# Polysketch attention and a top-2 router: plain scatters to a row per pair, one pass of sums, four blocks of the largest expert last

## The chip, the cores and the metric

One Trainium2 chip, one of its cores. The metric is the device time of one execution in microseconds (us); lower is better. Engines are named as in the profile: PE (TensorE), DVE (VectorE), ACT (ScalarE), POOL (GpSimd, which also issues the indirect DMAs), SP (SyncE, which issues the loads).

## The reference, cut to what matters

```python
x = polysketch_attention(q, k, v, S1, S2)         # 4 batches, 4 heads, 1088 tokens -> x [N=4352, D=128]
noisy = x @ w_gate + log1p(exp(x @ w_noise)) * noise          # [4352, E=8]
top2, top2_w = two largest per token, softmax over the two
out = zeros(N, D)
for e in range(8):                                # w1[e] is 128x1024, w2[e] is 1024x128, all float32
    for k in range(2):
        mask = top2[:, k] == e
        out[mask] += top2_w[mask, k] * (relu(x[mask] @ w1[e]) @ w2[e])
```

Each token sends two (token, expert) pairs, 8,704 in all, and a token's output is the sum of its two pairs' results.

## The kernel before, in words

The kernel has two stages. In the first, `attention` runs over the four batches, and after each group of four tiles of 128 tokens `router` picks the two experts of every token. For each pair it works out a row of the DRAM table `xs` (each expert has a region of its own there) and scatters 128 rows at a time to it: the token's input times its weight, and the token's number as a 129th word. Those are 68 indirect DMAs on POOL's queue (line 433), each of 128 rows of 516 bytes.

In between, `table` counts the pairs of each expert and cuts them into 27 large blocks (256 rows) and 21 small ones (128 rows). `ends` writes 128 filler rows behind each expert's last pair (eight DMAs on SP, line 518), whose token numbers point at 128 spare rows of the result.

In the second stage `blocks` works through the 48 blocks: large and small in turn 21 times, then six large ones. For each, `fetch` loads on SP the rows (`xb`, line 526) and the expert's two weight matrices (`w`, 512 KB each, lines 529 and 530), whichever expert it is; the pool behind these tiles has five buffers. `block_input` transposes the rows (line 545), line 584 makes `hp = w1.T x`, `evict` applies relu on ACT and DVE in turn (`h`, lines 537 and 539), and `second` (line 559) accumulates `acc = h.T w2`, two groups behind. `second` then copies `acc` to `y` and issues one or two scatters (line 568), each of which adds 128 rows of `y` to the rows of `total` that the 129th words of `xb` name. Two such scatters can hit the same row, so the program puts each behind the landing of the one before. An `xb` buffer is free again only when the scatter that reads its 129th words has landed. Before the first of the last six blocks stores its result, line 564 copies `total` to `out`, and the last 12 scatters add to `out` itself.

A scheduler (the tile framework) sets the order on each engine. It inserts the waits from what each instruction reads and writes. DMAs of one kind take eight semaphores in turn (DMASW0 to 7 for POOL's, DMAHW0 to 7 for SP's and ACT's), and a DMA that takes a semaphore waits for the DMA that had it eight DMAs before.

Of the kernel before, what the change touches and what calls it, by code (L numbers as in the profile page):

```python
# [8 lines left out]
F32 = mybir.dt.float32  # L9
# [12 lines left out]
def kernel(  # L22
# [49 lines left out]
    wpool = ctx.enter_context(tc.tile_pool(name="wpool", bufs=5))  # L72
    dram = ctx.enter_context(tc.tile_pool(name="dram", bufs=1, space=DRAM))
# [125 lines left out]
    for e in range(E):  # L199
        nc.gpsimd.memset(base[:, e:e + 1], float(e * CAP))  # L200
    token = const.tile([P, TILES], I32, name="token")
    nc.gpsimd.iota(token[:, 0:B * NT].rearrange("p (b t) -> p b t", b=B),
                   pattern=[[S, B], [1, NT]], base=0, channel_multiplier=NT)
    for c in range(2):
        nc.gpsimd.iota(token[HALF * c:HALF * (c + 1), B * NT:TILES], pattern=[[2 * S, 2]],
                       base=SM + S * c, channel_multiplier=1)
# [3 lines left out]

    pad = const.tile([P, XW], F32, name="pad")
    nc.gpsimd.memset(pad[:], 0.0)
    nc.gpsimd.iota(pad[:, D:XW].bitcast(I32), pattern=[[0, 1]], base=N, channel_multiplier=1)
    total = dram.tile([N + P, D], F32, name="total", tag="total")

    def clear():

        for r0 in range(0, N + P, 2 * P * 8):
            n = min(2 * P * 8, N + P - r0)
            nc.scalar.dma_start(total[r0:r0 + n, :].rearrange("(p r) d -> p (r d)", p=P),  # L220
                                zeros[:, 0:n * D // P])
        for c in range(2):
            nc.scalar.dma_start(xs[E * CAP + P * c:E * CAP + P * (c + 1), :], pad[:])
# [120 lines left out]
    def router(x, n, t0):  # L344
# [76 lines left out]
        for i, g in enumerate((g1, g2)):  # L421
# [6 lines left out]
            nc.gpsimd.tensor_copy(xg[:, 0:n, D:XW].bitcast(I32), token[:, t0:t0 + n].unsqueeze(2))  # L428
# [3 lines left out]
            for t in range(n):  # L432
                nc.gpsimd.indirect_dma_start(  # L433
                    out=xs[:], out_offset=bass.IndirectOffsetOnAxis(ap=to[:, t:t + 1], axis=0),
                    in_=xg[:, t, :], in_offset=None)


    def table():
# [27 lines left out]
        full = shifted("full", cnt, 8)  # L466
# [5 lines left out]
        V.scalar_tensor_tensor(out=left[:], in0=big[:], scalar=-2.0 * P, in1=cnt, op0=ALU.mult, op1=ALU.add)  # L472
        V.tensor_scalar_add(left[:], left[:], P - 1.0)
        rest_ = shifted("rest", left[:], 7)
        which = const.tile([1, NK], F32, name="which")
        first_row = const.tile([1, NK], F32, name="first_row")
        number = row("number", NB)
        num_i = row("num_i", NB, I32)
        nc.gpsimd.iota(num_i[:], pattern=[[1, NB]], base=0, channel_multiplier=0)
        V.tensor_copy(number[:], num_i[:])  # L480
        for name, lo, n, size, x in (("b", 0, NB, 2 * P, big), ("s", NB, NS, P, rest_)):
            end = sums("end" + name, x)
            past = row("past" + name, n * E)
            p3 = past[:].rearrange("p (i e) -> p i e", e=E)
            V.tensor_tensor(out=p3, in0=number[:, 0:n].unsqueeze(2).to_broadcast([1, n, E]),
                            in1=end[:, 1:E + 1].unsqueeze(1).to_broadcast([1, n, E]), op=ALU.is_ge)
            V.tensor_reduce(out=which[:, lo:lo + n], in_=p3, axis=AX.X, op=ALU.add)

            step = row("step" + name, E)
            V.tensor_scalar(out=step[:], in0=x[:], scalar1=-float(size), scalar2=float(CAP), op0=ALU.mult, op1=ALU.add)  # L490
            if name == "s":
                V.scalar_tensor_tensor(out=step[:], in0=big[:], scalar=-2.0 * P, in1=step[:], op0=ALU.mult, op1=ALU.add)
                V.scalar_tensor_tensor(out=step[:, 0:E - 1], in0=big[:, 1:E], scalar=2.0 * P, in1=step[:, 0:E - 1], op0=ALU.mult, op1=ALU.add)
            V.tensor_tensor(out=p3, in0=p3, in1=step[:].unsqueeze(1).to_broadcast([1, n, E]), op=ALU.mult)
            V.tensor_reduce(out=first_row[:, lo:lo + n], in_=p3, axis=AX.X, op=ALU.add)
            V.scalar_tensor_tensor(out=first_row[:, lo:lo + n], in0=number[:, 0:n], scalar=float(size),
                                   in1=first_row[:, lo:lo + n], op0=ALU.mult, op1=ALU.add)

        V.tensor_scalar(out=left[:, 0:1], in0=big[:, 0:1], scalar1=2.0 * P, scalar2=None, op0=ALU.mult)
        V.tensor_scalar(out=first_row[:, NB:NK], in0=first_row[:, NB:NK], scalar1=left[:, 0:1], scalar2=None, op0=ALU.add)  # L500
        V.tensor_scalar(out=first_row[:], in0=first_row[:], scalar1=float(E * CAP), scalar2=None, op0=ALU.min)
        V.tensor_scalar(out=which[:], in0=which[:], scalar1=float(E - 1), scalar2=None, op0=ALU.min)
        tab = const.tile([1, 2 * NK + E], I32, name="tab")
# [3 lines left out]
        V.tensor_tensor(out=tab[:, 2 * NK:2 * NK + E], in0=cnt, in1=base[0:1, :], op=ALU.add)  # L507
# [4 lines left out]

    def ends(tab):
        for e in range(E):
            at = 2 * (NB + NS) + e
            r = nc.values_load(tab[0:1, at:at + 1], engines=SP, min_val=0, max_val=E * CAP - P,
                               skip_runtime_bounds_check_because=IN_RANGE)
            nc.sync.dma_start(xs[bass.ds(r, P), :], pad[:])

    def fetch(tab, k, n):  # L520
        e = nc.values_load(tab[0:1, 2 * k:2 * k + 1], engines=SP, min_val=0, max_val=E - 1,
                           skip_runtime_bounds_check_because=IN_RANGE)
        r = nc.values_load(tab[0:1, 2 * k + 1:2 * k + 2], engines=SP, min_val=0, max_val=E * CAP,
                           skip_runtime_bounds_check_because=IN_RANGE)
        xb = wpool.tile([P, 2, XW], F32, name="xb", tag="xb")
        nc.sync.dma_start(xb[:, 0:n, :], xs[bass.ds(r, P * n), :].rearrange("(c p) d -> p c d", p=P))
# [4 lines left out]
        return xb, w1, w2  # L531
# [18 lines left out]
    def blocks(tab, order, copy_at):  # L550
        later, copied = [], []

        def second():
            acc, h, w2, n, js, j0, xb, to = later.pop(0)
# [7 lines left out]
            if j0 + js == FJ:  # L562
                if to is out and not copied:
                    copied.append(nc.scalar.dma_start(out, total[0:N, :]))
                y = moe.tile([P, 2 * D], F32, name="y", tag="y")
                evict(y[:, 0:D * n], acc[:, 0:D * n])
                for c in range(n):
                    nc.gpsimd.indirect_dma_start(  # L568
                        out=to[:], out_offset=bass.IndirectOffsetOnAxis(ap=xb[:, c, D:XW].bitcast(U32), axis=0),
                        in_=y[:, D * c:D * (c + 1)], in_offset=None, compute_op=ALU.add)  # L570

        data = [fetch(tab, *order[0])]
        xTs = [block_input(data[0][0], order[0][1])]
        for s_, (k_, n) in enumerate(order):
            xb, w1, w2 = data.pop(0)
            xT = xTs.pop(0)
            if s_ + 1 < len(order):
                data.append(fetch(tab, *order[s_ + 1]))
            acc = ps_o.tile([P, 2 * D], F32, name="acc", tag="acc")
            js = 4 // n  # L580
            for j0 in range(0, FJ, js):
# [6 lines left out]
                later.append((acc, h, w2, n, js, j0, xb, out if s_ >= copy_at else total))  # L588
# [76 lines left out]
```

## Time and profile before

| | |
|---|---|
| median of 2 runs | 794.75 us (792.77 to 796.72) |
| the profiled execution | 801.78 us, its span 800.1 us |
| PE busy | 498.1 us, 62% of the span, granted clock 0.799 of full speed on the mean |
| POOL, DVE, ACT busy | 212.6, 192.4 and 119.1 us |
| DMA | 77.25 MB, mean 97 GB/s |

The profiled execution has its own time; shares and places below are of its span. A DMA-issuing instruction on POOL is shown with the time POOL spends on it, not with the time until its data has landed. Idle time of an engine counts only where that engine is on the path that sets the end.

### The profile page before, as it was taken

How to read it: one execution, taken by the hardware profiler on the slowest of the kernel's cores; microseconds unless marked ns; L12 is line 12 of the kernel's file. 1: busy time of each engine (PE TensorE's matmuls, PEld its weight loads, DVE VectorE, ACT ScalarE, POOL GpSimd, SP SyncE). 2: the span in 40 equal slices, each digit the busy share in tenths (PEclk: the TensorE clock that was granted, in tenths of full speed). 3: DMA queues.
4: the chain of work that ended last, by engine and by line, in shares of the span. 5: the costliest groups of instructions: out<-in, count | busy, mean ns of one | idle time of the engine just before them, and what ended most of it. 6: DMA issues, size and time to landing. Idle time of an engine off the chain costs nothing. (4 is left out here: it accounts for less than half of the span.)

```text
span 800.1 us, 8013 instructions
## 1 busy us (share of the span) xinstructions
PE 498.1 (62%) x2781; PEld 422.4 (53%) x2781; DVE 192.4 (24%) x664; ACT 119.1 (15%) x232; POOL 212.6 (27%) x233
## 2 busy tenths in 40 slices
PE   1485585678557555009966667777667776771970
PEld 1363473465355333009966666666656765661960
DVE  2114513341441435402211111211111111110210
ACT  0112202301221222001211111111111111110110
POOL 3101332423233042301322223232232223222233
PEclk9995556655655655558999999999999999996895
DMA  7600100000000000028566565556556455656621
GB/s 187 224 28 4 46 14 17 17 17 17 10 23 24 0 23 21 27 84 235 133 158 148 145 162 129 130 140 160 134 136 175 127 129 138 162 138 164 188 30 17
DMA packets 95128, 77.25 MB, mean 97 GB/s; under 512 B 11632, under 2 KB 87536, under 8 KB 94768
## 3 DMA queue, kind: packets, MB, share of 16 engines
q1 hardware_dynamic: 74688, 62.12, 27.7%
q0 software_dynamic: 12976, 9.42, 7.6%
q10 hardware_dynamic: 7424, 5.21, 2.1%
q8 instruction: 22, 0.36, 0.2%
q14 instruction: 18, 0.15, 0.1%
HBM read 64.36 MB, written 14.59 MB: 99 GB/s over the span
## 5 line engine op out<-in xcount | busy, mean ns | idle before, releaser
L584 PE MATMUL hp<-bT,w 128*128 128x256 f32 (+1 forms) x768 | 165.2, 349 | 35.3 <-DMA w<-in_moe_w_dram 34.1
L568 POOL DMA_INDIRECT total<-y,xb x63 | 98.1, 1557 | 296.8 <-issue 108.3
L559 PE MATMUL acc<-w,h 128*128 128x128 f32 x1200 | 164.1, 282 | 16.1 <-ACT h L539 16.1
L559 PEld LDWEIGHTS acc<-w,h 128*128 128x128 f32 x1200 | 160.2, 198 | 22.5 <-ACT h L539 16.5
L584 PEld LDWEIGHTS hp<-bT,w 128*128 128x128 f32 x768 | 120.8, 200 | 48.1 <-issue 24.3
L433 POOL DMA_INDIRECT xs<-xg,to x68 | 68.3, 1005 | 169.0 <-DMA xs<-xg,to 80.7
L537 DVE TENSOR_SCALAR h<-hp 128x512 f32<-128x512 f32 x80 | 55.3, 692 | 232.6 <-PE hp L584 231.4
L545 PE MATMUL bank<-ident,xb 128*128 128x128 f32 x75 | 18.8, 310 | 98.9 <-DMA xb<-xs 98.9
L539 ACT ACTIVATE h<-hp 128x512 f32<-128x512 f32 x70 | 41.8, 597 | 227.8 <-PE hp L584 205.4
L545 PEld LDWEIGHTS bank<-ident,xb 128*128 128x128 f32 x75 | 9.0, 145 | 105.9 <-DMA xb<-xs 70.2
L415 PE MATMUL bank<-masks,earlier 128*128 128x32 f32 (+1 forms) x18 | 5.4, 394 | 62.9 <-DVE g L407 62.9
L415 PEld LDWEIGHTS bank<-masks,earlier 128*128 128x128 f32 x18 | 4.5, 310 | 63.6 <-issue 63.6
L316 PE MATMUL bank<-qT,sq 128*128 128x512 f32 (+1 forms) x36 | 30.9, 955 | 9.8 <-ACT qT L314 9.7
L284 PE MATMUL bank<-vaug,phk 128*128 128x66 f32 x128 | 29.3, 424 | 12.3 <-DVE phk L229 12.3
L235 PE MATMUL bank<-sk,kT 128*128 128x64 f32 x136 | 29.8, 419 | 9.0 <-ACT kT L270 8.5
L284 PEld LDWEIGHTS bank<-vaug,phk 128*128 128x128 f32 x128 | 27.9, 330 | 13.4 <-issue 9.8
L235 PEld LDWEIGHTS bank<-sk,kT 128*128 128x128 f32 x136 | 29.6, 333 | 9.7 <-ACT kT L270 8.9
L537 DVE COPY bT<-bank 128x256 f32<-128x256 f32 x21 | 8.9, 425 | 104.6 <-PE bank L545 104.6
L568 POOL DMA_INDIRECT out_dram<-y,xb x12 | 18.7, 1555 | 43.8 <-issue 26.3
L317 PE MATMUL bank<-qT,sq 128*128 128x512 f32 (+1 forms) x36 | 28.3, 883 | 0.0
L321 DVE TENSOR_TENSOR phq<-qa,bank 128x512 f32<-128x512 f32 (+1 forms) x18 | 11.8, 658 | 61.0 <-PE bank L317 61.0
L330 PEld LDWEIGHTS bank<-kv,phq 128*128 128x128 f32 (+1 forms) x144 | 17.9, 198 | 11.2 <-DVE phq L321 5.1
(157 smaller groups left out, 388.1 us busy)
## 6 DMA issues: line engine op xcount, KB each, us to landing
w<-in_moe_w_dram SPq DMA_DIRECT2D x96, 512.0 KB, 5.2
xb<-xs SPq DMA_DIRECT2D x27, 129.0 KB, 2.2
out_dram<-total ACTq DMA_DIRECT2D x1, 2176.0 KB
kld<-in_k_dram SPq DMA_DIRECT2D x4, 512.0 KB, 6.9
vld<-in_v_dram SPq DMA_DIRECT2D x4, 512.0 KB, 5.0
qld<-in_q_dram SPq DMA_DIRECT2D x4, 512.0 KB, 6.0
total<-zeros ACTq DMA_DIRECT2D x2, 1024.0 KB
xb<-xs SPq DMA_DIRECT2D x21, 64.5 KB
```

Source lines behind the costliest of these rows:

```text
L235: nc.tensor.matmul(ps[:, c0:c0 + H * 2 * R], lhsT=kT, rhs=sk[:, i, :], start=(i == 0), stop=(i == 1))
L284: nc.tensor.matmul(o, lhsT=phk[:, t, hs, :].rearrange("p h f -> p (h f)"), rhs=vaug[:, hs, t, :], start=(t == 0), stop=False)
L316: nc.tensor.matmul(pa[:, 0:w], lhsT=sq[:, 0, :], rhs=qT[:, 0:w], start=True, stop=True)
L317: nc.tensor.matmul(pb[:, 0:w], lhsT=sq[:, 1, :], rhs=qT[:, 0:w], start=True, stop=True)
L330: nc.tensor.matmul(ps[rows, c0:c0 + 2 * A1], lhsT=phq[hp][:, P * i + rows.start:P * i + rows.stop], rhs=kv[:, hp, :], start=True, stop=True)
L433: nc.gpsimd.indirect_dma_start(out=xs[:], out_offset=bass.IndirectOffsetOnAxis(ap=to[:, t:t + 1], axis=0), in_=xg[:, t, :], in_offset=None)
L537: nc.vector.tensor_scalar_max(o, i, 0.0) if relu else nc.vector.tensor_copy(o, i)
L539: nc.scalar.activation(out=o, in_=i, func=AF.Relu) if relu else nc.scalar.copy(o, i)
L545: nc.tensor.transpose(ps[:, P * c:P * (c + 1)], xb[:, c, 0:D], ident[:])
L559: nc.tensor.matmul(acc[:, D * c:D * (c + 1)], lhsT=h[:, P * (n * i + c):P * (n * i + c + 1)], rhs=w2[:, j, :], start=(j == 0 and c == 0), ...
L568: nc.gpsimd.indirect_dma_start(out=to[:], out_offset=bass.IndirectOffsetOnAxis(ap=xb[:, c, D:XW].bitcast(U32), axis=0), in_=y[:, D * c:D * ...
L584: nc.tensor.matmul(hp[:, P * n * i:P * n * (i + 1)], lhsT=w1[:, P * (j0 + i):P * (j0 + i + 1)], rhs=xT[:, 0:P * n], start=True, stop=True)
```

## The change

- The pairs' rows in `xs` now carry the pair's number (twice the token's, plus 0 or 1) in place of the token's. Every pair's result has a row of its own in a DRAM table `parts` of 8,704 rows, so the scatters of `y` are plain writes, declared free of each other; a row number past the table (filler rows) is dropped. The router's scatters to `xs` and the filler rows are declared free of each other too.
- `clear` now zeroes all of `parts`, 8,704 rows (five DMAs, 4.46 MB) in place of 4,480 rows of `total` (three DMAs, 2.29 MB).
- `table` finds the expert with the most pairs (`star`) and sets its first 1,024 rows aside as four large blocks; the rest is cut into 23 large and 21 small ones. The four are last in the order, and their weights are loaded once.
- When the first of the four is through, `combine` adds the two rows of each token in seven chunks of 5 rows a partition (SP loads `two`, DVE adds, SP stores `one` to `out`), and the four blocks' eight scatters add to `out` behind that.
- `xb` and `y` have pools of eight buffers of their own.

```diff
-    total = dram.tile([N + P, D], F32, name="total", tag="total")
+    parts = dram.tile([PAIRS, D], F32, name="parts", tag="parts")
+    def disjoint(group, i):
+        if group in groups:
+            tc.declare_no_dep(i.ins, group=group, reason="rows of their own")
+        tc.add_to_no_dep_group(group, i.ins)
+        groups.setdefault(group, []).append(i.ins)
+    def behind(i, group):
+        for w in groups[group]:
+            tc.add_manual_dep(i.ins, w.name, SYNC, reason="reads what they write")
...
     def clear():
-        for r0 in range(0, N + P, 2 * P * 8):
+        for r0 in range(0, PAIRS, 2 * P * 8):
...
-                nc.gpsimd.indirect_dma_start(
+                disjoint("xs", nc.gpsimd.indirect_dma_start(
                     out=xs[:], out_offset=bass.IndirectOffsetOnAxis(ap=to[:, t:t + 1], axis=0),
-                    in_=xg[:, t, :], in_offset=None)
+                    in_=xg[:, t, :], in_offset=None))
...
+        V.tensor_reduce(out=top[:], in_=cnt, axis=AX.X, op=ALU.max)
+        V.tensor_tensor(out=star[:], in0=cnt, in1=top[:].to_broadcast([1, E]), op=ALU.is_equal)
...
+            disjoint("xs", nc.sync.dma_start(xs[bass.ds(r, P), :], pad[:]))
...
+        i = nc.sync.dma_start(xb[:, 0:n, :], xs[bass.ds(r, P * n), :].rearrange("(c p) d -> p c d", p=P))
+        if not ready:
+            behind(i, "xs")
...
+        w1, w2 = weights(e)
+        return [(rows(r + 2 * P * i, n), w1, w2, n, True) for i in range(NL)]
...
+    def combine():
+        R_ = 5
+        per = N // P
+        src = parts[:].rearrange("(p r c) d -> p r c d", p=P, c=2)
+        dst = out.rearrange("(p r) d -> p r d", p=P)
+        for r0 in range(0, per, R_):
+            n = min(R_, per - r0)
+            two = cpool.tile([P, R_, 2, D], F32, name="two", tag="two")
+            behind(nc.sync.dma_start(two[:, 0:n], src[:, r0:r0 + n]), "parts")
+            one = cpool.tile([P, R_, D], F32, name="one", tag="one")
+            nc.vector.tensor_add(out=one[:, 0:n], in0=two[:, 0:n, 0, :], in1=two[:, 0:n, 1, :])
+            disjoint("out", nc.sync.dma_start(dst[:, r0:r0 + n, :], one[:, 0:n]))
...
-                if to is out and not copied:
-                    copied.append(nc.scalar.dma_start(out, total[0:N, :]))
+            if last and "out" not in groups:
+                combine()
+            y = ypool.tile([P, 2 * D], F32, name="y", tag="y")
+            if last:
+                tok = small.tile([P, 2, 1], U32, name="tok", tag="tok", bufs=4)
+                nc.vector.tensor_scalar(out=tok[:], in0=to, scalar1=1, scalar2=None, op0=ALU.logical_shift_right)
+            for c in range(n):
+                if last:
+                    i_ = nc.gpsimd.indirect_dma_start(
+                        out=out, out_offset=bass.IndirectOffsetOnAxis(ap=tok[:, c, :], axis=0),
+                        in_=y[:, D * c:D * (c + 1)], in_offset=None, compute_op=ALU.add)
+                    behind(i_, "out")
+                else:
+                    disjoint("parts", nc.gpsimd.indirect_dma_start(
+                        out=parts[:], out_offset=bass.IndirectOffsetOnAxis(ap=to[:, c, :], axis=0),
+                        in_=y[:, D * c:D * (c + 1)], in_offset=None, bounds_check=PAIRS - 1,
+                        oob_is_err=False))
...
+    order.append((None, 2))
```

Where the stages meet, POOL's queue before has the last router scatters to `xs` and the first block scatters to `total`; what each waits for stands in brackets. Counting from the first scatter, the four to `xs` at the end here have DMASW0 to DMASW3 as their own, and the first two to `total` have DMASW4 and DMASW5.

```order
L433 DMA xs<-xg_1739,to_1737 36096x129 [waits DMASW7_49,DVE_49,Pool_49]
L433 DMA xs<-xg_1739,to_1737 36096x129 [waits DMASW0_49]
L433 DMA xs<-xg_1749,to_1747 36096x129 [waits DMASW1_49,DVE_49,Pool_49]
L433 DMA xs<-xg_1749,to_1747 36096x129 [waits DMASW2_49]
L568 DMA total<-y,xb 4480x128 [waits DMAHW2_49,DMAHW1_49,DMAHW7_49,DMAHW0_49,DVE_49]
L568 DMA total<-y,xb 4480x128 [waits DMASW4_49]
L568 DMA total<-y,xb 4480x128 [waits DMAHW2_49,DMASW5_49,Activation_49]
```

Each waits for the semaphore of the scatter just before it. The same place now, with the same semaphores in turn:

```order
L453 DMA xs<-xg_1753,to_1751 36096x129 [waits DMASW0_49,DVE_49,Pool_49]
L453 DMA xs<-xg_1753,to_1751 36096x129 [waits DMASW1_49]
L453 DMA xs<-xg_1763,to_1761 36096x129 [waits DMASW2_49,DVE_49,Pool_49]
L453 DMA xs<-xg_1763,to_1761 36096x129 [waits DMASW3_49]
L657 DMA parts<-y,xb 8704x128 [waits DMAHW2_49,DMAHW3_49,DMAHW1_49,DMAHW4_49,DMASW4_49,DVE_49]
L657 DMA parts<-y,xb 8704x128 [waits DMASW5_49]
L657 DMA parts<-y,xb 8704x128 [waits DMAHW4_49,DMASW6_49,Activation_49]
```

Each now waits only for its own semaphore, that is, for the scatter eight before it.

On DVE the end of the program before is copies of `bT` and `y` and the relu of `h`:

```order
L537 COPY bT<-bank 128x256
L537 COPY y<-acc 128x256
L537 TENSOR_SCALAR h<-hp 128x512 x3
L537 COPY bT<-bank 128x256
L537 COPY y<-acc 128x256
L537 TENSOR_SCALAR h<-hp 128x512 x17
L537 COPY y<-acc 128x256
```

Now, from the shifts of the four last blocks' row numbers (`tok`) on; the ten `h` in a row end with the second group of the second of the four blocks:

```order
L644 TENSOR_SCALAR tok<-xb 128x2 x4
L588 COPY bT<-bank 128x256
L588 COPY y<-acc 128x256
L588 TENSOR_SCALAR h<-hp 128x512 x10
L614 TENSOR_TENSOR one<-two 128x640
L588 TENSOR_SCALAR h<-hp 128x512
L614 TENSOR_TENSOR one<-two 128x640
L588 TENSOR_SCALAR h<-hp 128x512
L614 TENSOR_TENSOR one<-two 128x640
L588 TENSOR_SCALAR h<-hp 128x512
L614 TENSOR_TENSOR one<-two 128x640
L588 TENSOR_SCALAR h<-hp 128x512 x2
```

All four `tok` stand ahead of the transposed rows (`bT`) of the first of the six last large blocks, and the sums of `combine` stand between the relus of the second to fourth of the four.

SP's queue before ends with the load of the last block; now it goes on from the rows of the four blocks to `combine`:

```order
L568 DMA xb<-xs 128x2x129 [waits DMAHW2_49,DMASW7_49]
L612 DMA two<-parts 128x1280 [waits DMASW4_49,DMASW5_49,DMASW3_49,DMASW6_49,DMASW2_49,DMAHW3_49,DMASW1_49,DMASW0_49]
L612 DMA two<-parts 128x1280 [waits DMAHW4_49]
L615 DMA out_dram<-one 128x640 [waits DMAHW5_49,DVE_49]
L612 DMA two<-parts 128x1280 [waits DMAHW6_49,DMAHW3_49]
L615 DMA out_dram<-one 128x640 [waits DMAHW7_49,DVE_49]
L612 DMA two<-parts 128x1280 [waits DMAHW4_49,DMAHW0_49]
```

The first load of `two` waits for every scatter to `parts`, and each later one stands behind the store of the sum before it.

## Rows read from the trace of the kernel before

**Rows 1.** Line 568, the result scatters: durations min/median/max in ns, first and last start
```profile
L568 POOL DMA_INDIRECT total<-y,xb x63: 1553/1557/1612, 372.4 to 730.8; - x63
L568 POOL DMA_INDIRECT out_dram<-y,xb x12: 1553/1556/1558, 747.9 to 793.3; - x12
...
DMA to landing us min/median/max: 3.2/5.7/6.9
```

**Rows 2.** SP's waits: line, whom it waited for, us in total, times, longest
```profile
SPq L526 <- DMA total<-y,xb: 268.2, 45, 12.1
...
SPq L518 <- DMA xs<-xg,to: 16.7, 1, 16.7
```

**Rows 3.** Windows: busy us of PE, PEld, DVE, ACT, POOL, then clock, DMA, GB/s
```profile
369.40:380.33 10.93, 10.93 (x86) 10.52 (x85) 2.93 (x5) 2.27 (x6) 3.20 (x2) 1.00 0.58 141
...
500.80:600.00 99.20, 68.90 (x465) 62.58 (x465) 16.33 (x29) 12.74 (x28) 26.47 (x17) 0.97 0.57 141
```

**Rows 4.** Timeline, weight loads on PE: start us, us, what, idle before
```profile
369.40 0.25 PEld L545 LDWEIGHTS bank<-ident,xb 128*128 128x128 f32 x2
...
380.33 0.26 PEld L545 LDWEIGHTS bank<-ident,xb 128*128 128x128 f32 x2
...
714.40 0.20 PEld L545 LDWEIGHTS bank<-ident,xb 128*128 128x128 f32 x2 [2.22 <-DMA xb<-xs]
```

**Rows 5.** DMA queues from 500 to 600 us: packets, MB, share
```profile
q1 hardware_dynamic: 15541, 12.81, 46.6%
q0 software_dynamic: 2448, 1.12, 10.3%
```

**Rows 6.** DMA queues from 355 to 372 us, the first five blocks' loads
```profile
q1 hardware_dynamic: 6055, 5.26, 100.9%
```

**Rows 7.** Timeline of ACT at the start: zeroing, and the copy behind it
```profile
24.43 1.60 ACTq L220 DMA_DIRECT2D total<-zeros  x2
...
28.96 0.58 ACT L270 COPY kT<-bank 128x512 f32<-128x512 f32 x1 [4.59 <-issue]
```

**Rows 8.** The window of that zeroing, columns as in rows 3
```profile
25.00:30.00 5.00, 0.40 (x2) 0.40 (x3) 0.10 (x1) 0.58 (x1) 0.00 (x0) 1.00 1.01 381
```

**Rows 9.** Timeline between the stages: count, table, first fetch, first block
```profile
320.96 0.17 DVE L446 COPY count<-bank 128x8 f32<-128x8 f32 x1 [0.28 <-PE bank L444]
...
329.56 0.18 DVE L506 CAST tab<-first_row 1x48 int32<-1x48 f32 x1
...
354.23 0.42 SPq L526 DMA_DIRECT2D xb<-xs  x1
355.15 0.36 SPq L529 DMA_DIRECT2D w<-in_moe_w_dram  x1
...
359.50 5.46 PE L584 MATMUL hp<-bT,w 128*128 128x256 f32 x12 [2.28 <-DMA w<-in_moe_w_dram]
```

**Rows 10.** Timeline of SP alone, the eight filler DMAs
```profile
338.86 13.65 SPq L518 DMA_DIRECT2D xs<-pad  x8
```

**Rows 11.** Line 433, the router's scatters, as rows 1
```profile
L433 POOL DMA_INDIRECT xs<-xg,to x68: 957/957/2902, 74.8 to 336.6; - x68
...
DMA to landing us min/median/max: 2.3/2.3/4.3
```

**Rows 12.** Timeline of the last large blocks on PE
```profile
738.28 2.07 PE L559 MATMUL acc<-w,h 128*128 128x128 f32 x8 [16.07 <-ACT h L539]
...
756.43 0.25 PEld L545 LDWEIGHTS bank<-ident,xb 128*128 128x128 f32 x2
...
763.68 0.25 PEld L545 LDWEIGHTS bank<-ident,xb 128*128 128x128 f32 x2
...
764.87 1.05 PE L559 MATMUL acc<-w,h 128*128 128x128 f32 x8
```

**Rows 13.** Groups by form on DVE: count, busy us, mean ns
```profile
L430 DVE TENSOR_TENSOR xg<-x,g 128x512 f32<-128x512 f32 x16 | 10.9, 687 | 0.1
```

**Rows 14.** Line 529, loads of 512 KB
```profile
DMA to landing us min/median/max: 3.8/4.0/4.2
```

More of the change, by code (lines that the diff above doesn't have):

```diff
@@ L471, in table @@
         V.tensor_tensor(out=big[:], in0=big[:], in1=full[:], op=ALU.min)
-        V.scalar_tensor_tensor(out=left[:], in0=big[:], scalar=-2.0 * P, in1=cnt, op0=ALU.mult, op1=ALU.add)
+        V.scalar_tensor_tensor(out=left[:], in0=big[:], scalar=-2.0 * P, in1=own[:], op0=ALU.mult, op1=ALU.add)
         V.tensor_scalar_add(left[:], left[:], P - 1.0)
-        rest_ = shifted("rest", left[:], 7)
-        which = const.tile([1, NK], F32, name="which")
-        first_row = const.tile([1, NK], F32, name="first_row")
+        small_ = shifted("small", left[:], 7)
@@ L548, in block_input, with blocks, more @@
         return xT
-    def blocks(tab, order, copy_at):
-        later, copied = [], []
+    def combine():
+        R_ = 5
+        rest_ = N - P * (N // P)
+        assert rest_ == 0
+        per = N // P
[8 more added lines that the diff above has]
+            disjoint("out", nc.sync.dma_start(dst[:, r0:r0 + n, :], one[:, 0:n]))
+    def blocks(tab, order):
+        later = []
+        todo = list(order)
+        data = []
+        def more():
+            if not data and todo:
+                data.extend(fetch(tab, *todo.pop(0)))
         def second():
-            acc, h, w2, n, js, j0, xb, to = later.pop(0)
+            acc, h, w2, n, js, j0, xb, last = later.pop(0)
             for i in range(js):
@@ L576, in blocks @@
+        more()
+        xTs = [block_input(data[0][0], data[0][3])]
+        while data:
+            xb, w1, w2, n, last = data.pop(0)
             xT = xTs.pop(0)
-            if s_ + 1 < len(order):
-                data.append(fetch(tab, *order[s_ + 1]))
+            more()
             acc = ps_o.tile([P, 2 * D], F32, name="acc", tag="acc")
@@ L587, in blocks @@
                 evict(h[:], hp[:], relu=True)
-                later.append((acc, h, w2, n, js, j0, xb, out if s_ >= copy_at else total))
+                later.append((acc, h, w2, n, js, j0, xb, last))
                 if len(later) > 2:
                     second()
-                if j0 + 2 * js == FJ and s_ + 1 < len(order):
-                    xTs.append(block_input(data[0][0], order[s_ + 1][1]))
+                if j0 + 2 * js == FJ and data:
+                    xTs.append(block_input(data[0][0], data[0][3]))
         while later:
@@ L631 @@
         order += [(i, 2)] * (i < NB) + [(NB + i, 1)] * (i < NS)
-    blocks(tab, order, copy_at=2 * NS)
+    order.append((None, 2))
+    blocks(tab, order)
 _INS = ['q', 'k', 'v', 'S1', 'S2', 'moe_w_gate', 'moe_w_noise', 'moe_noise', 'moe_w1', 'moe_w2']
```

128 lines of the change are left out of this document (76 added, 52 removed).

## Prediction

> **What bounds the kernel now.** Start with the windows of the second stage [rows 3]. Early on, from 369.40 to 380.33 us, PE is busy for all of the 10.93 us at full clock, and in that time exactly one large and one small block pass: the same transposes stand at 369.40 and 380.33 us [rows 4]. Later, from 500.80 to 600 us, PE is busy 68.90 of 99.20 us. The twentieth marker after the first stands at 714.40 [rows 4], so a pair of blocks takes 345.0 / 20 = 17.25 us on the mean where PE alone could do 10.93. Something else sets the pace for 20 pairs.
>
> The waits of SP say what [rows 2]: the loads of `xb` waited 268.2 us, 45 times, for result scatters to land. The scatters run from 372.4 to 730.8 us, 63 of them [rows 1], 5.8 us apart, three to a pair: 17.3 us, the pair's period. POOL itself is busy only 1.56 us with each; the rest is landing (median 5.7 us). So the chain is scatter, landing, next scatter. PE merely starves behind it, because an `xb` buffer comes free only when its scatter has landed, and the weights are queued behind `xb` on SP. The first pairs escape because five blocks are loaded ahead.
>
> **What the change does to that chain.** In the built order each scatter to `parts` waits only for the semaphore it shares with the scatter eight before, and `xb` and `y` have eight buffers. What is late next? In PE's favour: its 10.93 us a pair. POOL: three plain scatters; 128 rows to `xs` cost 0.957 us each [rows 11], an adding one 1.56 us [rows 1], so 2.9 to 4.7 us a pair. ACT and DVE are busy 2.27 and 2.93 us a pair [rows 3]. The DMA engines: from 500 to 600 us loads took 46.6% and scatters 10.3% of their time [rows 5], which is 0.569 x 17.25 = 9.8 us a pair. When the first five blocks were fetched, 5.26 MB came in 17 us, 309 GB/s [rows 6]; a pair's two sets of weights and rows are 2.30 MB, 7.4 us at that rate. All are below 10.93. I take PE as the new bound, with the DMA engines at 70 to 90%: 20 x (17.25 - 10.93) = **126.4 us saved** from the first marker to the last.
>
> **The start.** `clear` writes 2.17 MB more from ACT's queue. ACT's own copy of `kT` already stood 4.59 us behind those issues [rows 7], and PE's first products wait for it, so this lies on the path. DMA was full then, at 381 GB/s [rows 8]: 2.17 / 0.381 = **+5.7 us**. The ends are +0.7 (two more issues, if the queue took them) and +10 (half the rate while the inputs of the next batch come in).
>
> The router's scatters no longer wait for each other, yet in that stage POOL was behind nobody's wait that PE sat out; only the end of the stage gains. POOL's copies of `qx` and `kx` now stand behind eight scatters instead of one or two, 8 x 0.957 = 7.7 us later at most. They are made most of a batch ahead of the products that read them, so I cost this at nothing; without that cover it would be up to 7.7 us a batch, of which three have such scatters ahead.
>
> **Between the stages.** Before: count at 320.96, table done at 329.74, but the last router scatter starts only at 336.6 [rows 11], the eight filler DMAs run one behind the landing of the other for 13.65 us from 338.86 [rows 10], `xb` goes at 354.23 and the first block's product at 359.50 [rows 9]. After: count at 320.96 + 5.7 = 326.7. The table gets eleven more DVE instructions, some in its serial chain; 63 took 8.78 us, so 1.5 to 2.4 us, say 2.0: done at 337.5. The filler DMAs start right after the count and go one per 0.92 us (the step from `xb` to the weights, 354.23 to 355.15, also one register load and one DMA [rows 9]): 7.4 us, done and landed under the table. The scatters are caught up at 0.957 us each. So the table ends last: `xb` some 0.8 us later at 338.3, and the first product 5.3 us after that as before, at 343.6. That is **15.9 us earlier** than 359.50, the 5.7 included.
>
> **The second stage.** First marker 9.9 us after the first product, as before: 353.5. Twenty pairs: 572.1. Half a small block to go (10.93 less a large block's 7.25, the step from 756.43 to 763.68 [rows 12], is 3.7): 573.9. Two ordinary large blocks, 14.5: the first of the four starts at 588.4.
>
> One new wait stands before that. DVE has the four `tok` ahead of the `bT` of the first of the six last blocks, so it sits until the rows of all four blocks are there. SP loads those behind the weights of the first of the four, whose buffer is that of five blocks earlier (the twentieth small one). That comes free half a block into the 21st large one, 3.6 us; six issues at about 0.5 us and the landing behind 1 MB of weights (some 5 us) make 11.6. DVE gets to `tok` about 1 us after that block's 7.25. PE waits for `bT` in turn: **+3**, from 0 to 5. The first of the four at 591.4.
>
> **The tail,** counted from there. PE needs 4 x 7.25 = 29.0 us. The last ordinary `y` is there half a block in, at 4.0; two scatters (2 to 3 us) and their landing (2.3, [rows 11]) bring it to 8.5 to 9. Then `two`: 655 KB a chunk; 512 KB landed in 4.0 us [rows 14], so 4.5. A sum of 640 columns on DVE is 687 x 640 / 512 = 0.86 us [rows 13]. With two buffers and the stores in between on SP, two chunks pass per 5.4 us: seventh sum at 9 + 5.4 + 3 x 5.4 = 30.6, its store landed at about 33. DVE's order holds the relus of the second to fourth block behind the sums; that costs PE 2 to 3 us, still under the sums. Then eight adding scatters at 1.56 us, unordered among themselves: the last starts at 33.5 + 7 x 1.56 = 44.4, and from the start of the last scatter to the end of the span it was 800.1 - 793.3 = 6.8 us [rows 1]: **51.2 us**. Before, the same stretch (714.40 to the end) took 85.7 us; now it takes 1.8 + 14.5 + 3 + 51.2 = 70.5.
>
> **Sum.** Span 591.4 + 51.2 = 642.6, against 800.1: 157.5 us less (126.4 + 15.9 + 15.2). The profiled execution took 801.78, the median of the runs is 794.75, so I take the difference from the median: **637 us**.
>
> **Rivals.** (1) *The DMA engines become the bound.* PE does wait for rows in the steady stretch even now [rows 4], and 9.8 of 10.93 us is not much room; against it, this figure includes today's adding scatters, and the engines held more when pressed [rows 6]. It costs nothing until the 9.8 us grow by 12%; if they grow by 28%, to 12.6 a pair, it is 20 x 1.7 = 34 us: 671. Chance 0.12. The Trainium skill (DMA: Bandwidth & Descriptors, "Issuing engines are not separate DMA queues") says that DMAs from all issuing engines end up on the same 16 engines and interleave; by that, scatters let loose take time from the loads, and this rival is where it would show.
>
> (2) *Start and tail dearer.* Zeroing at +10, adding scatters at 2.90 us, the longest of line 433 [rows 11], and PE at half clock (1.2 of 2.4 GHz) behind its gaps in the tail: after a 16 us gap, eight products took 2.07 us in place of 1.05 [rows 12]. At that pace the last two blocks need 14.5 us more, most of it under the sums and the first six adds: some 3 us. Together +18: 655. Chance 0.08. The Trainium skill (TensorE: Matmul & The Clock Gate, "Part 1: The HAM clock gate") says that an idle PE falls back to half its clock. By that rule the gaps in the tail cost those 3 us. The trace agrees for the 16 us gap; the gaps of about two us in the steady stretch [rows 4] left the clock at 0.97 [rows 3].
>
> (3) *The order stays.* If the scatters still went one behind another's landing at today's pace, the 126 us stay and only the other gains come: about 770. The built order speaks against it. Chance 0.03.
>
> (4) *Slower: the eight semaphores.* A scatter waits for the eighth before it, so a pair takes at least 3/8 of the time from issue to landing. The longest landing seen is 6.9 us [rows 1], which asks for 2.6 us a pair. It decides from 29 us on; at 50 us the pair is back at 18.8 us and the time at 795, at 55 us it is 830. Plain writes crowding eight deep beside the loads would have to be eight times slower than the adding ones. Chance 0.02.
>
> **How the numbers follow.** 0.75 for the forecast. The low end takes the zeroing free (-5), no wait for `tok` (-3) and a tail of 41 (-10): 619. The high end is rival 1, 671; beyond lie (3), (4) and parts of the others, under 2 in 10. Faster by over 2% (what a measurement of this kernel can tell from no change is about that) in the forecast, (1), (2) and most of (3): 0.96; the rest 0.02 and 0.02.
>
> **What the profile after would show.** Markers 10.9 us apart to the last pair, PE busy over 95% between them at full clock; SP's wait for result scatters nearly gone; the first product near 344; the eight adds on POOL 1.56 us apart, starting some 33 us after the first of the four blocks. A longer pair with PE waiting for `w` is rival 1; PE waiting for `bT` near 572 us is `tok`. Wrong would be a pair over 12 us, or a tail over 65.

## The result, and the profile after

| | before | after |
|---|---|---|
| median of the runs, us | 794.75 (792.77 to 796.72, 2 runs) | 638.77 (637.79 to 639.75, 2 runs) |
| profiled execution, us | 801.78 | 637.79 |
| its span, us | 800.1 | 636.1 |

The ratio is 0.8037, 95% interval 0.7937 to 0.8138. The forecast was 637, range 619 to 671. With more runs, taken with the experiments, the changed kernel stands at 640.16 us (6 runs) against 799.35 us (11 runs): 0.8002, 0.7970 to 0.8034.

The windows of the kernel after, from the first marker to the last (20 pairs), then from the first of the four blocks to 611 us, just ahead of PE's last products, and from there to the end:

```profile
core 0: us, PE busy (x) PEld busy (x) DVE busy (x) ACT busy (x) POOL busy (x), PEclk, DMA share, GB/s
346.96:565.51 218.55, 218.55 (x1663) 210.31 (x1661) 58.68 (x101) 46.42 (x101) 58.97 (x60) 1.00 0.77 236
582.63:611.00 28.37, 28.37 (x197) 26.72 (x196) 10.98 (x17) 5.19 (x12) 1.97 (x2) 1.00 0.59 205
611.00:636.10 25.10, 2.72 (x22) 2.33 (x21) 2.09 (x4) 0.41 (x1) 12.54 (x8) 0.66 0.36 65
```

Twenty pairs take 218.55 us, 10.93 each where it was 17.25 [rows 3, 4], and PE does not stop in them. The DMA engines are at 0.77. SP's waits, columns as in [rows 2]:

```profile
SPq L561 <- PE acc L632: 97.2, 38, 4.1
SPq L612 <- DMA parts<-y,xb: 24.8, 3, 17.6
SPq L560 <- PE hp L673: 14.7, 18, 0.9
...
SPq L568 <- DMA parts<-y,xb: 2.2, 2, 1.9
```

The loads of `xb` waited 268.2 us for scatters before; they wait 2.2 now, and SP waits for PE instead, which is what one wants of the bound.

Between the stages, PE and then SP of the kernel after, in order of time (they answer to [rows 9, 10]):

```profile
320.05 0.57 PE L464 MATMUL bank<-before,ones 128*128 128x8 f32 x2
334.59 0.66 PE L596 MATMUL bank<-ident,xb 128*128 128x128 f32 x2 [13.97 <-DMA xb<-xs]
337.28 5.41 PE L673 MATMUL hp<-bT,w 128*128 128x256 f32 x12 [2.03 <-DMA w<-in_moe_w_dram]
```

```profile
321.79 6.41 SPq L555 DMA_DIRECT2D xs<-pad  x8
332.26 0.42 SPq L568 DMA_DIRECT2D xb<-xs  x1
333.19 0.36 SPq L560 DMA_DIRECT2D w<-in_moe_w_dram  x1
```

The fillers take 6.41 us in place of 13.65 and start right behind the count; the first product comes 17.2 us behind the count's product (320.05), not 39.

ACT at the start (answers to [rows 7]), and POOL in the tail:

```profile
23.83 2.12 ACTq L240 DMA_DIRECT2D parts<-zeros  x3
...
25.99 2.72 ACTq L240 DMA_DIRECT2D parts<-zeros  x2
28.81 2.54 ACTq L243 DMA_DIRECT2D xs<-pad  x2
31.45 0.59 ACT L290 COPY kT<-bank 128x512 f32<-128x512 f32 x1 [6.21 <-issue]
```

```profile
588.39 0.98 POOL L657 DMA_INDIRECT parts<-y,xb  x1 [0.30 <-issue]
617.34 1.60 POOL L648 DMA_INDIRECT out_dram<-y,tok  x1 [27.97 <-DMA out_dram<-one]
619.24 1.60 POOL L648 DMA_INDIRECT out_dram<-y,tok  x1 [0.30 <-issue]
...
630.45 1.55 POOL L648 DMA_INDIRECT out_dram<-y,tok  x1 [0.30 <-issue]
```

POOL idles 28 us between its last plain scatter and the first add, waiting for the stores of the pass. That is POOL's longest single wait of the second stage, and the eight adds stand behind it.

### The profile page after: what moved, and what is told of

Its sections match the earlier page's. It is cut to its first block, busy times and chain, and to the rows that moved or that the text cites. A ratio compares the mean times of both kernels' runs of the same rounds, so it can differ in the third digit from the quotient of the medians.

```text
span 636.1 us, 8071 instructions
## 1 busy us (share of the span) xinstructions
PE 469.1 (74%) x2781; PEld 408.6 (64%) x2781; DVE 198.5 (31%) x687; ACT 119.3 (19%) x232; POOL 174.7 (27%) x236
## 3 DMA queue, kind: packets, MB, share of 16 engines
q1 hardware_dynamic: 73152, 65.66, 33.5%
## 4 chain that ended last, share of the span: by engine, by line
issue 36%; PE 28%; DVE 12%; POOL 9%; DMA 6%; ACT 5%; ACTq 2%; POOLq 1%; SPq 0%; DVEq 0%
POOL parts L657 8%; PE bank L336 5%; PE bank L304 5%; PE bank L255 4%; PE bank L337 4%; DMA two<-parts 3%; PE bank L374 3%; PE bank L350 2%; PE bank L331 2%; ACT L395 2%; DVE phk L249 1%; ACT qT L334 1%; POOL out_dram L648 1%; DVE x L358 1%; DVE phq L341 1%
## 5 line engine op out<-in xcount | busy, mean ns | idle before, releaser
L673 PE MATMUL hp<-bT,w 128*128 128x256 f32 (+1 forms) x768 | 157.9, 338 | 2.4 <-DMA w<-in_moe_w_dram 2.0
L632 PE MATMUL acc<-w,h 128*128 128x128 f32 x1200 | 158.2, 275 | 0.5 <-DVE h L588 0.5
L632 PEld LDWEIGHTS acc<-w,h 128*128 128x128 f32 x1200 | 154.2, 192 | 6.2 <-DVE h L588 0.6
L673 PEld LDWEIGHTS hp<-bT,w 128*128 128x128 f32 x768 | 116.5, 194 | 9.2 <-issue 2.4
L657 POOL DMA_INDIRECT parts<-y,xb x67 | 65.8, 983 | 196.6 <-DVE y L588 147.9
L255 PE MATMUL bank<-sk,kT 128*128 128x64 f32 x136 | 29.8, 419 | 11.8 <-ACT kT L290 11.3
L336 PE MATMUL bank<-qT,sq 128*128 128x512 f32 (+1 forms) x36 | 29.9, 928 | 9.8 <-ACT qT L334 9.7
L304 PEld LDWEIGHTS bank<-vaug,phk 128*128 128x128 f32 x128 | 27.9, 330 | 13.4 <-issue 9.8
L341 DVE TENSOR_TENSOR phq<-qa,bank 128x512 f32<-128x512 f32 (+1 forms) x18 | 11.8, 658 | 59.1 <-PE bank L337 58.9
L337 PE MATMUL bank<-qT,sq 128*128 128x512 f32 (+1 forms) x36 | 27.4, 857 | 0.0
L596 PE MATMUL bank<-ident,xb 128*128 128x128 f32 x75 | 16.3, 277 | 14.0 <-DMA xb<-xs 14.0
L334 ACT COPY qT<-bank 128x512 f32<-128x512 f32 (+1 forms) x18 | 10.1, 562 | 76.6 <-PE bank L331 76.6
L350 PE MATMUL bank<-kv,phq 128*128 128x66 f32 (+1 forms) x144 | 19.0, 285 | 3.4 <-DVE phq L341 3.4
```

The lines of the kernel that those rows point to most:

```text
L255: nc.tensor.matmul(ps[:, c0:c0 + H * 2 * R], lhsT=kT, rhs=sk[:, i, :], start=(i == 0), stop=(i == 1))
L304: nc.tensor.matmul(o, lhsT=phk[:, t, hs, :].rearrange("p h f -> p (h f)"), rhs=vaug[:, hs, t, :], start=(t == 0), stop=False)
L336: nc.tensor.matmul(pa[:, 0:w], lhsT=sq[:, 0, :], rhs=qT[:, 0:w], start=True, stop=True)
L337: nc.tensor.matmul(pb[:, 0:w], lhsT=sq[:, 1, :], rhs=qT[:, 0:w], start=True, stop=True)
L350: nc.tensor.matmul(ps[rows, c0:c0 + 2 * A1], lhsT=phq[hp][:, P * i + rows.start:P * i + rows.stop], rhs=kv[:, hp, :], start=True, stop=True)
L632: nc.tensor.matmul(acc[:, D * c:D * (c + 1)], lhsT=h[:, P * (n * i + c):P * (n * i + c + 1)], rhs=w2[:, j, :], start=(j == 0 and c == 0), ...
```

## The experiments

Theory: the order of the scatters, each behind the landing of the one before, made the 17.25 us. Rivals: their adding, and the number of buffers. Runs 1 to 8 are one execution each and are compared with the profiled execution of the changed kernel (637.8 us). That kernel's eight executions lie between 636.5 and 641.6 us, so a difference of a few us is read from the traces, not from the times.

**1. Plain, but in order.**

```diff
-  disjoint("parts", nc.gpsimd.indirect_dma_start(out=parts[:], ...))
+  i_ = nc.gpsimd.indirect_dma_start(out=parts[:], ...)
+  groups.setdefault("parts", []).append(i_.ins)
```

> The changed kernel with one thing put back: the plain scatters to `parts` go one behind the landing of the other. Theory A (the order of the scatters made the 17.25 us of a pair): the step from one scatter to the next is its time from issue to landing, so with the 4.8 us that a plain one takes beside the loads a pair needs 3 x 4.8 = 14.4 us, 20 x 3.5 = 70 us more: about 709 us, and SP waits for scatters again. Theory B (it was the adding: an ordered plain scatter lands in the 2.3 us seen in the router's stage): 3 x 2.3 = 6.9 us, less than PE's 10.93: 638 us, as the changed kernel. The point between is a landing of 3.6 us.

Measured: 693.5 us. POOL's scatters in the middle of it, and SP's wait:

```profile
504.93 0.98 POOL L657 DMA_INDIRECT parts<-y,xb  x1 [4.70 <-issue]
509.66 0.98 POOL L657 DMA_INDIRECT parts<-y,xb  x1 [3.75 <-DMA parts<-y,xb]
512.66 0.98 POOL L657 DMA_INDIRECT parts<-y,xb  x1 [2.01 <-issue]
518.09 0.98 POOL L657 DMA_INDIRECT parts<-y,xb  x1 [4.44 <-issue]
```

```profile
SPq L568 <- DMA parts<-y,xb: 160.4, 42, 6.8
```

Three steps take 13.2 us here; the mean step is (644.3 - 352.5) / 66 = 4.42 us. The first nine pairs still pass at 10.93 us, fed from eight buffers; the next eleven take 13.5 each: 246.46 us for the twenty (349.62 to 596.08), 27.9 more than the changed kernel. As much again goes at the end, 95.7 us behind the last marker in place of 70.6: the rows of the four last blocks come late, DVE sits in `tok`, and PE behind it:

```profile
620.49 2.08 PE L674 MATMUL hp<-bT,w 128*128 128x256 f32 x4 [22.18 <-DVE bT L588]
...
626.02 1.03 PE L674 MATMUL hp<-bT,w 128*128 128x256 f32 x4
```

So the order alone, with scatters that add nothing, costs 55.7 us: 27.9 in the pairs, 25.1 at the end, 2.7 in the start's spread (below). Theory A held in kind, but it had put all of its 70 us into the pairs and nothing at the end. Theory B falls. After 22 us of waiting the same four products take 2.08 us, and 1.03 a little later: the granted clock was 0.50 (1.2 GHz) from 612 to 622.6 us and 1.00 (2.4 GHz) from 626 on. The Trainium skill (TensorE: Matmul & The Clock Gate, "Part 1: The HAM clock gate") has an idle PE fall to half its clock; this run agrees, and the tail of the changed kernel never gave it the occasion: from the first of the four blocks to its last products PE waits 0.45 us in all, and the clock is 1.00 up to 611 us.

**2. Adding, but free.**

```diff
-  in_offset=None, bounds_check=PAIRS - 1, oob_is_err=False))
+  in_offset=None, bounds_check=PAIRS - 1, oob_is_err=False, compute_op=ALU.add))
```

> The changed kernel with one thing put back: the scatters to `parts` add (into zeroed rows, so the sums are the same), unordered as before. Theory A (order): POOL needs 3 x (1.56 + 0.30) = 5.6 us a pair, under PE's 10.93, so pairs stay at 10.93 us; the last scatter ends some 0.6 us later: 639 us. Theory B (adding): pairs well over 12 us, 670 us and more, with SP waiting for scatters or PE for weights.

Measured: 642.87 us. The pairs take 10.93 us (347.07 to 565.62 after, 348.69 to 567.25 here). The scatters, count, min/median/max in ns, first and last start:

```profile
L657 POOL DMA_INDIRECT parts<-y,xb x67: 1553/1557/1612, 351.6 to 591.1; - x67
```

Of the 5 us, 1.6 lie ahead of the table (the spread of the start, below). The rest is at the end: the last scatter starts 1.1 us later, the loads of `two` another 1.1 behind it, the first add another 0.6, and the last add takes 0.7 longer to the end. Theory A holds.

**3. The kernel before with eight buffers.**

```diff
-  xb = wpool.tile([P, 2, XW], F32, name="xb", tag="xb")
+  xb = wpool.tile([P, 2, XW], F32, name="xb", tag="xb", bufs=8)
-  y = moe.tile([P, 2 * D], F32, name="y", tag="y")
+  y = moe.tile([P, 2 * D], F32, name="y", tag="y", bufs=8)
```

> The kernel before with eight buffers for `xb` and for `y` in place of five and three, nothing else. Theory A (order): the chain scatter, landing, scatter runs on at 5.8 us a step; more blocks are loaded ahead, but the last scatter comes when it did: 795 to 800 us. Theory B (it was the number of buffers that made PE starve): pairs at 10.93 us, about 670 us.

Measured: 804.81 us, the kernel before beside it 800.89. SP's wait hardly moves, and the 63 scatters stretch from 374.5 to 741.4, 5.9 us a step:

```profile
SPq L526 <- DMA total<-y,xb: 248.6, 43, 10.2
```

Buffers alone bring nothing. With runs 1 to 3 the four corners are (where the order holds, the pairs behind the first ones, which pass at 10.93 us from the buffers):

| pair of blocks, us | adding | plain |
|---|---|---|
| in order, eight buffers | 17.6 (run 3, on the kernel before) | 13.5 (run 1) |
| free, eight buffers | 10.93 (run 2) | 10.93 (after) |

**4. The router's scatters and the fillers in order again.**

```diff
-  disjoint("xs", nc.gpsimd.indirect_dma_start(out=xs[:], ...))
+  i_ = nc.gpsimd.indirect_dma_start(out=xs[:], ...)
+  groups.setdefault("xs", []).append(i_.ins)
```

(and the same for the eight filler DMAs)

> The changed kernel with one thing put back: the router's scatters to `xs` and the eight filler DMAs go one behind the landing of the other. The prediction's term for the stretch between the stages: first product of the first block at 359 to 360 us in place of 337.3, the rest as in the changed kernel: 638 + 22 = 660 us. Rival: the table, not the order, sets that stretch; then the first product stays near 338 us and the time at 638 us.

Measured: 659.17 us. SP and PE:

```profile
339.56 12.61 SPq L556 DMA_DIRECT2D xs<-pad  x8
353.58 0.42 SPq L570 DMA_DIRECT2D xb<-xs  x1
```

```profile
358.49 3.75 PE L675 MATMUL hp<-bT,w 128*128 128x256 f32 x8 [1.99 <-DMA w<-in_moe_w_dram]
```

The count stands where it stood (321.0), the first product 21.2 us later, the end 21.4. This term of the sum is the order again, and it is whole. The run puts two orders back at once; the trace shows both: the last router scatter starts at 337.08 us in place of 325.91, and the fillers take 12.61 us in place of 6.41.

**5. Five and three buffers.**

```diff
-  xpool bufs=8, ypool bufs=8
+  xpool bufs=5, ypool bufs=3
```

> The changed kernel with five buffers for `xb` and three for `y`, as before the change, in place of eight and eight. Theory A (the buffers only had to be many because of the order; a plain scatter's 4.8 us of landing fits in the 10.93 us of a pair): the pairs stay at 10.93 us; only the loads of the last four blocks' rows may come later, 0 to 5 us: 638 to 643 us. Theory B (the buffers carry the gain): pairs of 12 us and more, 660 us and up.

Measured: 640.34 us, though its count came 2.3 us early. The pairs stay at 10.93 us (344.67 to 563.22). SP waits 127.2 us for scatters again, and PE does not notice until the last four blocks' rows, 11.8 us for a block that takes 7.24 (a wait of 2.65 us, and behind it a granted clock of 0.55 from 575.4 to 578.4 us, where it is 1.00 in the changed kernel):

```profile
SPq L568 <- DMA parts<-y,xb: 127.2, 23, 8.0
```

```profile
574.39 1.16 PE L632 MATMUL acc<-w,h 128*128 128x128 f32 x8 [2.65 <-DVE h L588]
```

Theory A holds: the buffers are worth some 5 us, all of it at the four last blocks. SP's wait in the rows of a profile says nothing by itself; PE's does.

**6. Less work on PE.**

```diff
   j = j0 + i
+  if 0 < j < FJ - 1:
+      continue
```

> The changed kernel with six of the eight products of each block's second layer left out (only the first and the last of the inner index are computed, so the output is not the reference's). PE then needs about 10.93 x (0.5 + 0.125) = 6.8 us a pair. It shows the bound behind PE. If the DMA engines come next by the prediction's 9.8 us a pair: 20 x 1.1 us saved, about 615 us. If they manage the 309 GB/s seen when five blocks were fetched, 7.4 us a pair: 20 x 3.5 = 71 us saved, about 565 us, less some of the tail. If the DMA engines were full already, as rival 1 had it, nothing is saved: 638 us.

Measured: 572.77 us; pairs of 8.03 us (348.78 to 509.58 for 20). The window of fifteen of them:

```profile
389.11:509.58 120.47, 111.57 (x707) 99.00 (x706) 43.89 (x75) 34.83 (x75) 44.22 (x45) 1.00 1.00 313
```

The DMA engines are at 1.00 with 313 GB/s. One could take them for the next bound, but the waits say otherwise. PE's one wait in this window is for DVE's copy of the transposed rows, 0.5 us a pair, none is for a DMA, and SP waits for PE to give weight buffers free:

```profile
PE hp L674 <- DVE bT L588: 7.8, 15, 0.5
```

```profile
SPq L561 <- PE acc L633: 26.3, 14, 1.9
```

Nor is 313 GB/s their ceiling: in the five pairs before this window they moved 346.

```profile
348.78:389.11 40.33, 37.88 (x245) 33.93 (x244) 15.05 (x26) 12.21 (x26) 14.76 (x15) 1.00 1.10 346
```

So 8.03 us is still the pace of PE with the copies and relus between its products (PE busy 0.93 of the time), and the DMA engines need at most that for a pair, 2.9 us under the changed kernel's 10.93. Which of them is next behind PE isn't shown. Rival 1 was thus further off than the prediction had it. The Trainium skill (DMA: Bandwidth & Descriptors, "Issuing engines are not separate DMA queues") has the DMAs of all issuing engines interleave on the same 16; loads and scatters together did keep these busy all the time here, and PE still waited for none of them.

**7 and 8. What the zeroing costs.** Run 7 zeroes `parts` twice; run 8 zeroes it once in DMAs of half the size.

```diff
-  for r0 in range(0, PAIRS, 2 * P * 8):
-      n = min(2 * P * 8, PAIRS - r0)
+  for r0 in range(0, PAIRS, 2 * P * 4):
+      n = min(2 * P * 4, PAIRS - r0)
```

> The changed kernel with the zeroing of `parts` done twice: five more DMAs and 4.46 MB more on ACT's queue ahead of its copy of `kT`. Theory A (the prediction's price, bytes on the path at 381 GB/s): the copy of `kT` comes 11.7 us later and so does the count: 649 to 650 us. Theory B (ACT waits only for room in its queue, and PE's phases at half and at full clock take a delay of up to 2.5 us back): `kT` some 6 us later, 2.5 us for two DMAs more being the one measured step, the count 3 to 6 us later: 641 to 644 us.

> The changed kernel with the zeroing of `parts` in nine DMAs of at most 0.5 MB in place of five of at most 1 MB: the same rows and bytes, four more issues on ACT's queue ahead of its copy of `kT`. Theory B (the copy waits for the issues, some 1.3 us for each when the queue is full): `kT` at 36 to 37 us in place of 31.4, the count near 327 us, 643 us. Theory A (the bytes): `kT` at 31 to 32 us, the count within 318 to 324 us, 638 us.

Run 7: 655.57 us, above both theories. It doesn't tell them apart: ACT issued two zeroings from 23.71 on and seven in 13.33 us from 30.94 on, 1.9 us each, and `kT` came at 46.95. I take it that a second write of the same rows waits for the landing of the first; the trace does not name that wait. Run 8: 647.1 us, with

```profile
24.06 2.10 ACTq L240 DMA_DIRECT2D parts<-zeros  x3
26.19 7.67 ACTq L240 DMA_DIRECT2D parts<-zeros  x6
33.96 2.17 ACTq L243 DMA_DIRECT2D xs<-pad  x2
36.23 0.59 ACT L290 COPY kT<-bank 128x512 f32<-128x512 f32 x1 [10.74 <-DMA parts<-zeros]
```

Same bytes, four issues more, `kT` 4.8 us later: 1.2 us an issue, as Theory B had it. Theory A falls. (The last three issues also wait for the landing of the DMA eight before them, which may be a part of it; the six ahead go at 7.67 / 6 = 1.28 us, near the 2.72 / 2 = 1.36 of the changed kernel.) The count came at 329.1, 8.4 us later than in the changed kernel's profile, and the end 9.3: more than `kT` itself, and what made up the rest isn't shown.

**9. The loads of the pass first,** and **10.** with the sums on POOL.

```diff
+  for r0 in range(0, per, R_):      # R_ = 4, was 5; `one` has four buffers, was two
+      two = ...                     # six buffers of the first stage's inputs and two of its own
+      behind(nc.sync.dma_start(two[:, 0:n], src[:, r0:r0 + n]), "parts")
+      twos.append((r0, n, two))
+  for r0, n, two in twos:
       one = cpool.tile([P, R_, D], F32, name="one", tag="one")
-      nc.vector.tensor_add(...)
+      nc.vector.tensor_add(...)     # run 10: nc.gpsimd.tensor_add(...)
```

> The changed kernel with all nine loads of `two` (four rows a partition each, eight buffers, six of them those of the first stage's inputs) issued ahead of the sums and stores; nothing else moves. Theory: the eight last adds wait for the last store, and that store waits for the two buffers of the pass. 4.46 MB then land in 10.6 us (at the 420 GB/s of the zeroing) to 14.4 us (at 309), so the adds start 3 to 8 us before 617.3, and the end comes 3 to 8 us earlier: 630 to 635 us in place of 637.8. Rival: the sums are held by DVE's order among the relus of the last blocks, so they end where they ended: 637 us. A second rival: DVE then holds the relus behind the sums, PE waits, and it is 640 us.

> As the run with the loads first, and the nine sums on POOL, which does nothing between its last scatter to `parts` and the first add to `out`. If DVE's order holds the sums back there, this one starts the adds at 606 to 610 us and ends 7 to 11 us before the changed kernel: 627 to 631 us. If the landing of the loads and stores sets the time, both runs give the same. If POOL's sums are slow (over 2 us each), the adds start no earlier than 612 us: 633 us and more.

> The changed kernel once more, beside the runs of this call: 638 us, its count within 318 to 324 us as in the runs so far.

| six executions each | median, us | ratio to before |
|---|---|---|
| loads first | 634.73 | 0.7934 (0.7905 to 0.7962) |
| and sums on POOL | 637.18 | 0.7962 (0.7932 to 0.7992) |
| the changed kernel again | 640.16 | 0.8002 (0.7970 to 0.8034) |

The loads first are faster than the changed kernel by 5.4 us in the medians, under 1%, with intervals that do not touch. In the profiles it is 2.7 us (span 635.6 against 638.3, counts 322.9 and 322.7; first add at 616.73 against 619.40), but the profiled execution of run 9 is the slowest of its six. By the medians that is the middle of the 3 to 8 us that I expected, by the adds just short of it. It is the lowest median, though run 11 is within its interval. The sums on POOL bring nothing: 637.18 us, the interval overlaps that of run 9, and the 627 to 631 us that DVE's order would have meant did not come. The sums of runs 9 and 10 (DVE, POOL):

```profile
601.57 0.69 DVE L622 TENSOR_TENSOR one<-two 128x512 f32<-128x512 f32 x1
...
608.61 0.69 DVE L622 TENSOR_TENSOR one<-kld 128x512 f32<-128x512 f32 x1 [1.00 <-DMA out_dram<-one]
```

```profile
600.87 1.27 POOL L622 TENSOR_TENSOR one<-two 128x512 f32<-128x512 f32 x1
608.16 1.27 POOL L622 TENSOR_TENSOR one<-kld 128x512 f32<-128x512 f32 x1 [6.02 <-DMA out_dram<-one]
```

On both engines four sums run by 602, and the fifth starts at 608, when a store of `one` has landed: `one` has four buffers, and beside the loads its stores take up to 9.7 us in run 9 (2.0 for the last, alone). The place of the wait moved from `two` to `one`. More buffers for `one`, or sums in place, were not tried.

**11. No blocks kept for the end,** the pass after all blocks, no zeroing of `parts`.

```diff
-  NL = PAIRS // E // (2 * P)
+  NL = 0
-  order.append((None, 2))
```

> One part of the change left out: no blocks of the largest expert are kept for the end (27 large and 21 small blocks, each pair's row written to `parts`), the pass with its nine loads first comes after all blocks, no adds to `out`. As every row of `parts` is then written, it is not zeroed. Theory A (the four last blocks pay): the pass lies bare behind the last block, 612 + 5 us of scatters and landing, 13 to 17 us of loads, 4 us of last sum and store: 637 us by itself, less what the start gains. Theory B for the start (ACT's queue: five fewer issues at about 1.3 us each bring `kT` 6 us earlier, and the count too): 628 to 633 us in all. If the zeroing costs the end nothing, 636 to 640 us.

Measured: 635.53 us, ratio 0.7944 (0.7913 to 0.7975): not to be told from the loads first with four blocks kept. It lies above the 628 to 633 us of Theory B and just under the 636 to 640 of a zeroing that costs nothing. Its start:

```profile
24.15 0.84 ACTq L239 DMA_DIRECT2D xs<-pad  x2
25.09 0.59 ACT L286 COPY kT<-bank 128x512 f32<-128x512 f32 x1 [0.94 <-DVE phk_rest L245]
```

`kT` is 6.1 us earlier than in run 9 (31.23), the count 8.8 (314.1 against 322.9). Behind PE's last product lie 25.3 us (606.4 to 631.7) against 19.0 (616.6 to 635.6). So keeping four blocks back saves about 6 us of bare pass, and the zeroing that it needs costs about as much at the start. Beside the loads first this part brings nothing that this case can show; with the change's own order of loads, leaving it out was not tried.

## Why the prediction was right, and which terms were off

The steps, in the prediction's order, spans of the two profiled executions:

- **20 pairs: right.** 126.4 us predicted, 345.0 - 218.55 = 126.45 measured. Cause shown by runs 1 to 3: the order of the scatters, with the adding as what makes each of its steps long. Put back alone, with plain scatters, the order costs the pairs 27.9 us (55.7 in all, with the end); the adding alone costs them nothing, and more buffers alone gain nothing. So the 126 us are those of adding scatters in order, 5.8 to 5.9 us a step, where plain ones in order take 4.42.
- **Between the stages: right.** From the count to the first product 16.9 us predicted (326.7 to 343.6), 16.6 measured (320.7 to 337.3). Run 4 puts it back: 21.2 us.
- **The start: mis-sized.** The step "2.17 / 0.381 = +5.7 us" took bytes for the price. `kT` came 2.5 us later (31.45 against 28.96), the price of two more issues on ACT's queue; run 8 shows the 1.2 us an issue with the bytes unchanged. The count of the changed kernel came no later at all (320.66 against 320.96). That is luck within a spread: nine profiles with this first stage, experiments among them, have it at 318.3 to 323.3, mean 321.9; two with the first stage of the kernel before at 321.0 and 321.7. Runs 8 and 11 moved it by 7 to 8 us with `kT`, so a delay there does reach the end; whether 2.5 us do on the mean isn't settled.
- **`tok`: mis-sized.** +3 predicted. DVE did sit for the rows of four blocks, until 567.60, but PE lost only 0.36 us to it. DVE's wait came about as reckoned (3.2 us in all before the four `tok`); the step that failed is that PE would sit it out in turn, for PE still had 16 products of the small block to do:

```profile
565.62 0.38 PE L596 MATMUL bank<-ident,xb 128*128 128x128 f32 x2
565.84 1.06 PE L673 MATMUL hp<-bT,w 128*128 128x128 f32 x8
566.73 1.06 PE L632 MATMUL acc<-w,h 128*128 128x128 f32 x8
568.15 1.13 PE L673 MATMUL hp<-bT,w 128*128 128x256 f32 x4 [0.36 <-DVE bT L588]
...
573.52 0.38 PE L596 MATMUL bank<-ident,xb 128*128 128x128 f32 x2
...
580.76 0.38 PE L596 MATMUL bank<-ident,xb 128*128 128x128 f32 x2
```

  The cost is real where the rows are later: 22 us in run 1, some 5 in run 5.
- **The tail: 51.2 predicted, 53.5 measured.** The pass came out close (last sum at 31.1 us, 30.6 predicted). The adds were taken at 1.56 us each; the step is 1.87, since POOL leaves 0.30 us between two: 7 x 0.31 = 2.2 us. Two smaller misses cancel: the first add came 34.7 us in, not 33.5, and the end 5.6 us behind the last add's start, not 6.8.

Together the span was forecast 6.5 us too long: -6.0 for the start, -2.6 for `tok`, +2.3 for the tail, the rest rounding. Its three terms of gain, 126.4, 15.9 and 15.2 us, measured 126.45, 22.2 and 15.1; the last agrees only because `tok` and the tail cancel. That 637 still lies 2 us from the median is partly chance: the two runs before had a median of 794.75, and eleven later ones 799.35. The difference, 157.5 us predicted, is 159.2 by the longer series.

Of the rivals, the DMA engines were not near the bound: at 8.03 us a pair PE still waited for no DMA (run 6). The order did go; the "about 770" given for its staying does not follow from its own terms (637 + 126 = 763), and nothing hangs on it. The eight semaphores never showed: the longest landing of a scatter to `parts` was 7.3 us, where 29 would have been needed.

## What to carry to other kernels

Where a loop runs slower than its busiest engine, divide the last minus the first start of each kind of DMA by its count: a step that equals time from issue to landing is a chain, and rows of their own let it go, adding or not. Before the DMA engines are called a bound, see what the busiest engine waits for: their share stood at 1.00 in run 6, and PE waited for none of them. DMAs ahead of an engine's next instruction on its own queue were paid here by the issue, not by the byte. When a pass behind the last scatter gets more buffers on its input, count those of its output too.

## What the runs showed that I had not expected

- On ACT, the zeroing DMAs behind the first three went at one per 1.28 us with 0.5 MB each (run 8) and one per 1.36 us with up to 1 MB (the changed kernel), the two small `xs<-pad` at one per 1.1 to 1.3 us, and the engine's next instruction stood behind them. I read that as a queue that is full; no run shows its room.
- The same first stage ends up to 5 us apart from profile to profile (the changed kernel's own two: 320.66 and 322.69). At one place the traces show how a difference goes: two products between the first and the second router product took 1.12 us after, at a granted clock of 1.00 (80.5 to 81.7 us, 2.4 GHz), and the very same ones before took 2.08, at 0.50 (78.39 to 80.5 us, 1.2 GHz):

```profile
80.56 1.12 PE L336 MATMUL bank<-qT,sq 128*128 128x512 f32 x2 [0.73 <-ACT qT L334]
```

```profile
78.39 2.08 PE L316 MATMUL bank<-qT,sq 128*128 128x512 f32 x2 [0.73 <-ACT qT L314]
```

  In this way most of the 2.2 us that the first group's router product was late (72.95 against 70.79) were gone, and all of them by the next one (96.09 against 96.04). That the clock makes the whole spread isn't shown.
- An adding scatter costs POOL 1.56 us where a plain one costs 0.98, and in order the pairs with adding scatters (17.6 us, run 3) take 4 us more than with plain ones (13.5, run 1); free, the adding costs the pairs nothing.
